# The first 384 tokens in tiles of 128 queries with all heads, up to product 1, and key zeros written by the evacuations

## The chip, the cores and the metric

One core of a Trainium2 chip. The metric is the device time of one execution in microseconds (us). The fast executions of one kernel lie within about 1.3% of each other here; runs that came out over 1.5% above the fastest of the same kernel are called slow. No ratio below uses them.

Names in the views: PE is TensorE (the matmuls), PEld its weight loads, DVE VectorE, ACT ScalarE, POOL GpSimd. Matmuls and transposes write into PSUM; an evacuation is a copy out of it. A load lands when its last byte has arrived and whoever waits for it is released.

## The reference, cut to what matters

Eight heads of causal attention over 768 tokens, four batches, head size 64. Heads 0, 2 and 6 see every earlier token; the others see the first four tokens (the sinks) and a window of 64. The result, 3072 tokens of 512 values, goes through two products with a leaky ReLU between them.

```python
scores = q @ k.T / sqrt(64)             # per batch and head
keep   = causal, or causal & (sink | in_window) for heads 1, 3, 4, 5, 7
x      = (softmax(where(keep, scores, -1e9)) @ v).transpose(0, 2, 1, 3).reshape(3072, 512)
h      = x @ w_in                       # product 1: 512 -> 2048
out    = maximum(0.01 * h, h) @ w_out   # product 2: 2048 -> 512
```

## The kernel before

It works through eight chunks of 384 tokens. While TensorE does the products of one chunk, the attention of the next is threaded into them. Only the first chunk has no products to hide behind, and its front is what the change rewrites. Keys are kept as `kt[partition, pair, head in pair, token]`: two heads share the 128 partitions, and the half that belongs to the other head must be zero, so that one matmul can contract over 128 partitions.

```python
def turn_pair(n, p, tags, engs, nms="kq"):       # one pair of heads, 384 tokens
    ...                                          # three transposes into PSUM tile pt
    if nm == "k":
        for hh in range(2):
            r = slice(64 * hh, 64 * hh + 64)     # only the head's own half
            move(kt[i][r, p, hh, CH * c : CH * c + CH], pt[r, 0:3, :])
    else:
        move(qx[n][:, p, :], pt[:, 0:3, :])

def zero_keys(i, eng, lo, hi):                   # the other halves
    for hh in range(2):
        eng.memset(kt[i][64 - 64 * hh : 128 - 64 * hh, :, hh, lo:hi], 0.0)

for p in range(2):
    load_pair("k", nc.sync, p)                   # heads 0 to 3 as fp32 pairs
    load_pair("q", nc.scalar, p)
make_identity(nc, ident)
load_three("k", nc.gpsimd, 4, 8)                 # heads 4 to 7 as bf16
load_three("q", nc.gpsimd, 4, 8)
...
for i in range(2):
    nc.vector.memset(va[i][:, :, :, D], 1.0)     # the ones column of v: first on DVE
nc.vector.memset(shift[:], 0.0)
nc.vector.tensor_copy(ident_f[:], ident[:])
zero_keys(0, nc.vector, 0, CH)
... # masks on POOL
load_v(0, (0,))                                  # after the ones in program order
...
zero_keys(1, nc.gpsimd, 0, CH)
...
turn_pair(0, 0, ("py", "py"), "va")              # then scores, exp, mask, v by head
...
p0 = in_slots(0)                                 # product 1 of the first chunk:
run(p0[0:1])                                     # 16 blocks of 4 matmuls of 384 columns
```

`va` is the v tile: 65 columns for each head, 64 of v and one of ones, which gives the sum of the softmax with the same matmuls. A load of v and the memset of the ones write different bytes of the same tile. `move` copies from PSUM with DVE ("v") or ACT ("a").

The softmax here doesn't subtract the row's maximum and nothing guards it: scores larger than these inputs give would overflow.

Of the kernel before, what the change touches and what calls it, by code (L numbers as in the profile page):

```python
# [21 lines left out]
def kernel(  # L22
# [36 lines left out]
    def bank(tag, shape, dtype):  # L59
        return ps.tile(shape, dtype, name=tag, tag=tag, bufs=BANKS[tag])  # L60

    def bf(name, *shape):
        return one.tile([128, *shape], BF16, name=name)

    wide = {nm: ap.rearrange("b h (c p g) d -> b c p h (g d)", g=3, p=128) for nm, ap in (("q", q), ("k", k))}
    nat = {nm: ap.rearrange("b h (c g p) d -> b c p h g d", g=3, p=128) for nm, ap in (("q", q), ("k", k), ("v", v))}
    q_k = {nm: ap[0, :, 0:CH].rearrange("h (g p) d -> p h g d", p=128) for nm, ap in (("q", q), ("k", k))}
    w_in_r = moe_w_in.rearrange("(g p) n -> p g n", p=128)
    w_out_r = moe_w_out.rearrange("(g p) n -> p g n", p=128)

    ident = bf("ident", 128)
    ident_f = one.tile([128, 128], FP32, name="ident_f")
    m_caus = bf("m_caus", 128)
    m_one = bf("m_one", 64)
    m_win = bf("m_win", 6, 64)
# [6 lines left out]
    vs = [bf(f"vs{i}", H, D + 1) for i in range(2)]  # L82
    ksink = [bf(f"ksink{i}", 4 * SK) for i in range(2)]
    ats = [bf(f"ats{i}", 3, 4, 64) for i in range(5)]
    w_in_bf = bf("w_in_bf", KG, DF)
    w_out_bf = bf("w_out_bf", NG, DM)


    raw = {}

    three = {}

    def load_three(nm, eng, lo, hi):
        t = one.tile([128, hi - lo, 3 * D], BF16, name=f"{nm}w{lo}")
        for h in range(lo, hi):
            three[nm, h] = t[:, h - lo]
        eng.dma_start(out=t[:], in_=wide[nm][0, 0, :, lo:hi])

    def load_pair(nm, eng, p):
        t = one.tile([128, 3, 2, D], FP32, name=f"{nm}f{p}")  # L100
        three[nm, p, "f"] = t
        for hh in range(2):
            eng.dma_start(out=t[:, :, hh], in_=q_k[nm][:, 2 * p + hh])

    def load_qk(n, nms="kq"):
        b, c = ORDER[n]
# [6 lines left out]
    def load_v(n, gs=range(3)):  # L113
        b, c = ORDER[n]
        for g in gs:
            nc.gpsimd.dma_start(out=va[b][:, 3 * c + g, :, 0:D], in_=nat["v"][b, c, :, :, g])  # L116
# [3 lines left out]
    def load_sinks(b):  # L120
        vsf[b] = rot.tile([32, D], FP32, name="vsf", tag="vsf", bufs=2)
        nc.sync.dma_start(out=vsf[b][:], in_=v[b, :, 0:NS, :])
# [9 lines left out]
    def load_in(c0, c1):  # L132
        nc.gpsimd.dma_start(out=w_in_bf[:, :, c0:c1], in_=w_in_r[:, :, c0:c1])
# [9 lines left out]
        eng.dma_start(out=vb[i][0:64, lo:hi], in_=va[i][64:128, lo:hi])  # L143
        eng.dma_start(out=vb[i][64:128, lo:hi], in_=va[i][0:64, lo + 1 : hi + 1])

    def v_shift_pe(t, tag, eng, b=0):
        s = bank(tag, [128, 512], FP32)
        w = 7 * (D + 1)
        for e in range(2):
            nc.tensor.matmul(s[:, 0:w], lhsT=shift[:, e, :], rhs=va[b][:, t + e, 1:H, :],  # L150
                             start=(e == 0), stop=(e == 1))
        dst, src = vb[b][:, t, 1:H, :], s[:, 0:w].rearrange("p (h d) -> p h d", h=7)
        if eng == "v":
            nc.vector.tensor_copy(dst, src)  # L154
        else:
            nc.scalar.activation(out=dst, in_=src, func=ACTF.Copy)
# [6 lines left out]
    def zero_keys(i, eng, lo, hi):  # L163
        for hh in range(2):
            eng.memset(kt[i][64 - 64 * hh : 128 - 64 * hh, :, hh, lo:hi], 0.0)  # L165

    def zero_small(i, eng):
        eng.memset(ksink[i][:], 0.0)
        eng.memset(vs[i][:], 0.0)
# [9 lines left out]
            return qx[n][:, g, p, lo - 128 * g : hi - 128 * g]  # L179
        return qx[n][:, g : hi // 128, p, :]  # L180

    def turn_pair(n, p, tags, engs, nms="kq"):
        b, c = ORDER[n]
        i = b % 2
        if n not in qx:
            qx[n] = rot.tile([128, 4, CH], BF16, name="qt", tag="qt", bufs=2)
        for nm, tag, eng in zip(nms, tags, engs):
            f = n == 0 and p < 2
            pt = bank(tag, [128, 4, 128], FP32 if f else BF16)
            for g in range(3):  # L190
                if f:
                    nc.tensor.transpose(pt[:, g, :], three[nm, p, "f"][:, g], ident_f[:])
                elif n == 0:
                    for hh in range(2):
                        nc.tensor.transpose(pt[64 * hh : 64 * hh + 64, g, :],
                                            three[nm, 2 * p + hh][:, D * g : D * g + D], ident[:])
                else:
                    nc.tensor.transpose(pt[:, g, :], raw[nm, n][:, g, 2 * p : 2 * p + 2, :], ident[:])

            def move(dst, src):  # L200
                if n == 0 and not f:
                    src = src.rearrange("p g t -> p t g")
                    dst = dst.rearrange("p (t g) -> p t g", g=3)
                else:
                    dst = dst.rearrange("p (g t) -> p g t", g=3)
                if eng == "v":
                    nc.vector.tensor_copy(dst, src)
                else:
                    nc.scalar.activation(out=dst, in_=src, func=ACTF.Copy)

            if nm == "k":
                for hh in range(2):
                    r = slice(64 * hh, 64 * hh + 64)
                    move(kt[i][r, p, hh, CH * c : CH * c + CH], pt[r, 0:3, :])
            else:
                move(qx[n][:, p, :], pt[:, 0:3, :])

    def turn_dma(n):
        qx[n] = rot.tile([128, 3, 4, 128], BF16, name="qd", tag="qd", bufs=3)
# [44 lines left out]
    def sink_keys(b):  # L264
        for f in sink_keys_by(b):
            f()
# [168 lines left out]
            return r  # L435


    gs = {}
    py = {}

    def in_slots(n, tags=("ph",)):
        def tick(t):
            if t == 0:
                gs[n] = rot.tile([128, NG, CH], BF16, name="g", tag="g", bufs=2)
            ph = bank(tags[t % len(tags)], [128, 512], FP32)
            for g in range(KG):
                nc.tensor.matmul(ph[:, 0:CH], lhsT=w_in_bf[:, g, 128 * t : 128 * t + 128],  # L447
                                 rhs=xts[n][:, g, :], start=(g == 0), stop=(g == KG - 1))
            nc.scalar.activation(out=gs[n][:, t, :], in_=ph[:, 0:CH], func=ACTF.Prelu, alpha=0.01)  # L449

        return [lambda t=t: tick(t) for t in range(NG)]

    def out_slots(n, tags=("py", "py", "py"), halves=False):
        slots = []
# [25 lines left out]
    def run(*lists):  # L480
        for l in lists:
            for f in l:
                f()

    def merge(ms, as_):

        r, done = [], 0
        for j, m in enumerate(ms):
            want = (j + 1) * len(as_) // len(ms)
            r += as_[done:want] + [m]  # L490
            done = want
        return r + as_[done:]


    for p in range(2):
        load_pair("k", nc.sync, p)
        load_pair("q", nc.scalar, p)
    make_identity(nc, ident)
    load_three("k", nc.gpsimd, 4, 8)
    load_three("q", nc.gpsimd, 4, 8)  # L500
    load_sinks(0)
    load_sinks(1)
    for i in range(2):
        nc.vector.memset(va[i][:, :, :, D], 1.0)
    nc.vector.memset(shift[:], 0.0)
    nc.vector.tensor_copy(ident_f[:], ident[:])
    zero_keys(0, nc.vector, 0, CH)
    for a in ats:
        nc.vector.memset(a[:, :, 1:3, :], 0.0)
    nc.scalar.activation(out=shift[:, 0, 0:64], in_=ident[:, 64:128], func=ACTF.Copy)  # L510
    nc.scalar.activation(out=shift[:, 1, 64:128], in_=ident[:, 0:64], func=ACTF.Copy)
    nc.gpsimd.memset(m_caus[:], 1.0)
    keep(m_caus[:], [[1, 128]], ALU.is_ge, 0, -1)
    load_v(0, (0,))
    nc.gpsimd.memset(m_one[:], 1.0)
    keep(m_one[:], [[-1, 64]], ALU.is_gt, 0, 1)
    keep(m_one[:], [[1, 64]], ALU.is_ge, 64, -1)
    load_v(0, (1, 2))
    load_in(0, 512)
    nc.gpsimd.memset(m_sink[:], 1.0)  # L520
    keep(m_sink[:], [[-NS, H]], ALU.is_ge, 0, 1)
    keep(m_sink[:], [[NS, H]], ALU.is_ge, NS - 1, -1)
    zero_small(0, nc.gpsimd)
    load_qk(1)
    zero_keys(1, nc.gpsimd, 0, CH)
    zero_small(1, nc.gpsimd)
    load_in(512, 1024)
    load_v(1)
    load_in(1024, 1536)
    load_in(1536, 2048)  # L530
    for i in range(3):
# [2 lines left out]
    load_out(3)  # L534
    load_v(2)

    a0 = Attention(0, ("psS", "ph"), ("po", "po", "py", "py"))
    R0, S1, R2, S3, S4, S5, R6, S7 = (a0.units[h] for h in range(H))

    def qk(*us):  # L540
        run([x[0] for x in us])

    def av(*us):
        run([x[1] for x in us])

    turn_pair(0, 0, ("py", "py"), "va")
    nc.vector.tensor_copy(m_win[:], m_one.rearrange("p (o t) -> p o t", o=1).to_broadcast([128, 6, 64]))
    nc.vector.tensor_copy(m_win0[:, 1:], m_win[:, 1:])
    nc.vector.tensor_copy(m_win0[:, 0, :], m_caus[:, 0:64])
    nc.vector.memset(m_win0[0:NS, 1, :], 1.0)  # L550
    qk(*R0)
    qk(*S1)
    turn_pair(0, 1, ("po", "po"), "av")
    turn_pair(0, 2, ("py", "py"), "va")
    qk(*R2)
    qk(*S3)
    turn_pair(0, 3, ("po", "po"), "av")
    sink_keys(0)
    qk(*R6)
    qk(*S4)  # L560
    v_shift_pe(0, "ph", "a")
    v_shift_pe(1, "psS", "v")
    av(*R0)
    qk(*S5)
    a0.sink()
    sink_values(0, nc.vector)
    nc.vector.tensor_copy(vs[0][0:32, :, D], m_sink[0:32, :])
    av(*R2)
    qk(*S7)
    av(*S1)  # L570
    xs0 = a0.finish(0)
    av(*S3)
    xs1 = a0.finish(1)
    av(*R6)
    av(*S4)
    av(*S5)
    xs2 = a0.finish(2)
    av(*S7)
    xs3 = a0.finish(3)
    a0.x_t(0, xs0, "ph")  # L580
    turn_pair(1, 0, ("psS",), "a", "k")
    a0.x_t(1, xs1, "ph")
    turn_pair(1, 1, ("psS",), "v", "k")
    a0.x_t(2, xs2, "ph")
    a0.x_t(3, xs3, "ph", "v")
    p0 = in_slots(0)
    run(p0[0:1])
    turn_pair(1, 0, ("psS",), "v", "q")
    turn_pair(1, 1, ("psS",), "a", "q")
    run(p0[1:2])  # L590
    turn_pair(1, 3, ("psS", "psS"), "va")
    run(p0[2:3])
    a1 = Attention(1, po_tags=("po", "po", "po", "py"), xt_eng="v").slots([0, 2, 6, 1, 3, 4, 5, 7])
    run(a1[0:2])
    turn_pair(1, 2, ("py", "py"), "va")
    sink_keys(1)
    sink_values(1, nc.vector)
    nc.vector.tensor_copy(vs[1][0:32, :, D], m_sink[0:32, :])


    shifts = [lambda: v_shift_pe(0, "ph", "v", 1), lambda: v_shift_pe(1, "ph", "v", 1)]
    run(p0[3:4], merge(p0[4:8], a1[2:7] + shifts[0:1] + a1[7:8] + shifts[1:]), merge(p0[8:12], a1[8:-3]), merge(p0[12:], a1[-3:]))
    zero_keys(0, nc.vector, CH, S)
    zero_keys(1, nc.vector, CH, S)
    for i in range(2, B):
# [72 lines left out]
```

## Time and profile before

| | before |
|---|---|
| time, median of 3 runs (range) | 242.64 us (242.45 to 243.33) |
| span of the profiled run | 241.4 us |
| first transpose | 4.33 us |
| first matmul of product 1 | 22.68 us |
| product 1 of the second 384 tokens begins ("the join") | 42.4 us |

In the slices of the span (40 of 6.0 us; a digit is the busy share in tenths), TensorE is less than 90% busy only in the first five, in one near the middle and in the last:

```profile
PE   2787899999999999899999999999999999999994
```

In the timeline, each line is: start in us, duration of one or of the whole group in us, engine, line and operation, what it writes and reads, how many; in brackets how long the engine stood before it and for what. Two lines of the kernel before: the ones of the v tile are the first thing on DVE, and the first load of v comes behind them:

```profile
1.05 0.31 DVE L504 MEMSET va<- 128x48 bf16 x2 [1.05 <-PEq L659]
...
3.67 0.90 POOL L116 DMA_DIRECT2D va<-in_v_dram  x1
```

The other views of the kernel before stand in the prediction.

### The profile page before, as it was taken

To read this page: it belongs to the slowest core of one execution; us is meant where nothing else is said; L and a number is where in the kernel's file an instruction comes from. 1 tells how busy PE (TensorE), PEld (TensorE's weight loads), DVE (VectorE), ACT (ScalarE), POOL (GpSimd) and SP (SyncE) were. 2 spreads that over 40 slices of the span, in tenths; PEclk is the share of its full clock that TensorE was granted. 3 is DMA by queue.
4 is the path that set the end of the run, shared out by engine and by line. 5 is a ranking of instruction groups with operands and counts; after the bars stand their busy time and mean duration, and the time that the engine had idled before them with its cause. 6 is when DMAs were issued, how large, how long until landed. Compare 5 with 4: busy or idle time off the path is not lost.

```text
span 241.4 us, 4947 instructions
## 1 busy us (share of the span) xinstructions
PE 226.1 (94%) x1980; PEld 137.0 (57%) x1980; DVE 97.6 (40%) x267; ACT 130.2 (54%) x286; POOL 74.6 (31%) x98
## 2 busy tenths in 40 slices
PE   2787899999999999899999999999999999999994
PEld 2555566554556567565656655666556665555553
DVE  6667547405254537327712671234511441111121
ACT  3664865660665687665436553766556764433300
POOL 8999734119239007705900840000000000000000
PEclk9999999999999999999999999999999999999999
DMA  7999999999999995996998999751210111111112
GB/s 127 184 162 114 190 207 176 178 151 151 138 187 206 191 182 35 141 177 140 133 148 129 188 172 105 159 124 30 69 55 7 61 35 60 43 43 46 42 45 87
DMA packets 107334, 29.08 MB, mean 120 GB/s; under 512 B 99248, under 2 KB 103600, under 8 KB 107312
## 3 DMA queue, kind: packets, MB, share of 16 engines
q0 software_dynamic: 73920, 13.24, 69.9%
q1 hardware_dynamic: 31792, 15.15, 31.0%
q10 hardware_dynamic: 1600, 0.39, 0.8%
q8 instruction: 15, 0.25, 0.4%
q14 instruction: 7, 0.06, 0.1%
HBM read 27.30 MB, written 6.29 MB: 139 GB/s over the span
## 4 chain that ended last, share of the span: by engine, by line
PE 83%; POOL 7%; DVE 4%; ACT 3%; DMA 1%; issue 1%; DVEq 0%; POOLq 0%
PE ph L447 34%; PE py L460 29%; PE po L292 6%; PE psS L323 5%; PE psS L460 4%; PE psS L358 2%; PE psS L303 2%; DMA out_dram<-o 1%; POOL kt L165 1%; POOL qb L111 1%; POOL kb L111 1%; POOL va L116 1%; ACT ats L363 1%; ACT xt L403 1%; PE psS L401 1%
## 5 line engine op out<-in xcount | busy, mean ns | idle before, releaser
L447 PE MATMUL ph<-xt,w_in_bf 128*128 128x384 bf16 x512 | 101.9, 325 | 0.4 <-DVE vb L154 0.3
L449 ACT ACTIVATE g<-ph 128x384 bf16<-128x384 f32 x128 | 63.0, 492 | 60.4 <-PE ph L447 59.5
L460 PE MATMUL py<-w_out_bf,g 128*128 128x512 bf16 (+1 forms) x352 | 91.0, 374 | 0.0
L447 PEld LDWEIGHTS <-w_in_bf 128*128 128x128 bf16 x512 | 46.6, 97 | 33.6 <-issue 2.2
L460 PEld LDWEIGHTS <-g 128*128 128x128 bf16 x400 | 35.4, 97 | 25.9
L328 ACT ACTIVATE at<-psS 128x384 bf16<-128x384 f32 x81 | 38.5, 491 | 16.2 <-PE psS L323 16.1
L466 DVE COPY o<-py 128x512 f32<-128x512 f32 (+1 forms) x22 | 14.9, 678 | 52.1 <-PE py L460 50.7
L111 POOL DMA_DIRECT2D kb<-in_k_dram x21 | 18.6, 895 | 32.8 <-DMA kd<-kb 32.1
L323 PE MATMUL psS<-qd,kt 128*128 128x384 bf16 (+2 forms) x90 | 22.9, 293 | 0.0
L367 DVE TENSOR_TENSOR ats<-ats,m_win 128x384 bf16<-128x384 bf16 x40 | 15.1, 377 | 17.7 <-ACT ats L363 17.3
L116 POOL DMA_DIRECT2D va<-in_v_dram x24 | 21.3, 910 | 2.4 <-DMA w_out_bf<-in_moe_w_out_dram 1.8
L292 PE MATMUL po<-va,at 128*128 128x65 bf16 x240 | 20.3, 195 | 1.4 <-DVE at L333 1.1
L363 ACT ACTIVATE ats<-psS 128x384 bf16<-128x384 f32 x38 | 18.5, 490 | 5.2 <-PE psS L358 4.9
L292 PEld LDWEIGHTS <-at 128*128 128x128 bf16 x252 | 16.2, 99 | 7.4 <-DVE at L333 1.5
L111 POOL DMA_DIRECT2D qb<-in_q_dram x21 | 18.6, 908 | 5.3 <-DMA w_out_bf<-in_moe_w_out_dram 2.4
L391 DVE TENSOR_TENSOR xs<-po,linv 128x384 bf16<-128x384 f32 x29 | 16.2, 557 | 1.0
L358 PEld LDWEIGHTS <-kt 128*128 128x128 bf16 x240 | 12.9, 102 | 6.5 <-issue 0.4
L333 DVE TENSOR_TENSOR at<-at,m_caus 128x128 bf16<-128x128 bf16 x24 | 5.6, 231 | 25.6 <-ACT at L328 25.5
L323 PEld LDWEIGHTS <-kt 128*128 128x128 bf16 x108 | 10.4, 99 | 9.4 <-issue 1.9
L231 DVE COPY kt<-kd 64x512 bf16<-64x512 bf16 x36 | 13.5, 374 | 0.6
L292 PEld LDWEIGHTS <-ats 128*128 128x128 bf16 x240 | 11.2, 97 | 4.0 <-DVE ats L367 0.8
L331 DVE TENSOR_TENSOR at<-at,m_caus 128x256 bf16<-128x256 bf16 x24 | 7.0, 291 | 14.2 <-ACT at L328 14.2
(107 smaller groups left out, 168.1 us busy)
## 6 DMA issues: line engine op xcount, KB each, us to landing
out_dram<-o SPq DMA_DIRECT2D x23, 256.0 KB, 3.6
va<-in_v_dram POOLq DMA_DIRECT2D x24, 128.0 KB, 6.9
kb<-in_k_dram POOLq DMA_DIRECT2D x21, 128.0 KB, 5.6
qb<-in_q_dram POOLq DMA_DIRECT2D x21, 128.0 KB, 5.8
w_in_bf<-in_moe_w_in_dram POOLq DMA_DIRECT2D x4, 512.0 KB, 7.4
w_out_bf<-in_moe_w_out_dram POOLq DMA_DIRECT2D x4, 512.0 KB, 12.7
vb<-va SPq DMA_DIRECT2D x8, 195.0 KB, 3.7
vb<-va SPq DMA_DIRECT2D x4, 130.0 KB, 3.1
```

Of the source, the lines that this page charges most:

```text
L111: nc.gpsimd.dma_start(out=t[:, g], in_=nat[nm][b, c, :, :, g])
L116: nc.gpsimd.dma_start(out=va[b][:, 3 * c + g, :, 0:D], in_=nat["v"][b, c, :, :, g])
L292: nc.tensor.matmul(o, lhsT=lhsT, rhs=rhs, start=first, stop=False, skip_group_check=True)
L323: nc.tensor.matmul(s[:, off : off + w], lhsT=kt[i][:, p, hh, 128 * kj : 128 * kj + 128], rhs=q_of(n, p, lo, CH), start=(j == 0), stop=(j = ...
L328: nc.scalar.activation(out=a[:, 0:off], in_=s[:, 0:off], func=ACTF.Exp, scale=SM)
L358: nc.tensor.matmul(s[:, 64 * m : 64 * m + 64], lhsT=kt[i][:, p, hh, k0 : k0 + 128], rhs=q_of(n, p, 64 * m, 64 * m + 64), start=(m == 0), s ...
L363: nc.scalar.activation(out=av_, in_=s[:, 0:CH].rearrange("p (j e f) -> p j e f", j=3, e=2), func=ACTF.Exp, scale=SM)
L367: nc.vector.tensor_mul(av_, av_, m_)
L391: nc.vector.tensor_tensor(xs[:], po[:, :, :, 0:D], linv.to_broadcast([128, 3, 2, D]), op=ALU.mult)
L447: nc.tensor.matmul(ph[:, 0:CH], lhsT=w_in_bf[:, g, 128 * t : 128 * t + 128], rhs=xts[n][:, g, :], start=(g == 0), stop=(g == KG - 1))
L449: nc.scalar.activation(out=gs[n][:, t, :], in_=ph[:, 0:CH], func=ACTF.Prelu, alpha=0.01)
L460: nc.tensor.matmul(py[n][:, 0 : c1 - c0], lhsT=gs[n][:, ng, 128 * tt : 128 * tt + 128], rhs=w_out_bf[:, ng, c0:c1], start=(ng == 0), stop= ...
```

## The change

The intent is a shorter front. The first 384 tokens are taken in three tiles of 128 queries, each with all eight heads, so that product 1 of tile 0 can begin before tiles 1 and 2 are through. Tile 0 of k and q comes as fp32 for all heads and is cast; the other tiles come as bf16. Thirteen matmuls on zeros (`idle`) are to warm TensorE. The zeros of the keys are no longer written by memsets: an evacuation of k copies the full 128 partitions, once for each head of the pair, multiplied by a per-partition scalar that is 1 on the head's own half and 0 on the other. The core of the diff:

```diff
-    for p in range(2):
-        load_pair("k", nc.sync, p)
-        load_pair("q", nc.scalar, p)
+    load_first("k")
+    load_first("q")
+    load_v(0, (0,))
     make_identity(nc, ident)
-    load_three("k", nc.gpsimd, 4, 8)
-    load_three("q", nc.gpsimd, 4, 8)
+    load_tile(1)
+    load_v(0, (1,))
     load_sinks(0)
     load_sinks(1)
+    nc.vector.memset(blank[:], 0.0)
+    ... # half: ones on a head's own partitions, zeros on the other
     for i in range(2):
         nc.vector.memset(va[i][:, :, :, D], 1.0)
     nc.vector.memset(shift[:], 0.0)
-    nc.vector.tensor_copy(ident_f[:], ident[:])
-    zero_keys(0, nc.vector, 0, CH)
+    ... # zeros of the sink keys, sink values and two mask tiles
+    nc.vector.tensor_copy(k0[:, 0], f0["k"])
+    nc.scalar.activation(out=q0[:, 0], in_=f0["q"], func=ACTF.Copy)
...
-    zero_keys(1, nc.gpsimd, 0, CH)
...
+def move(eng, dst, src, hh=None):
+    if eng == "v" and hh is None:  nc.vector.tensor_copy(dst, src)
+    elif eng == "v":               nc.vector.tensor_scalar_mul(dst, src, half[:, hh : hh + 1])
+    ... # the same two on ACT, with scale=
...
-    turn_pair(0, 0, ("py", "py"), "va")
-    ... # four pairs, scores by head, v, transposes of x
+    idle("psS", 13)
+    turn_tile("k", 0, "va"); turn_tile("q", 0, "v"); turn_tile("k", 1, "va")
+    F0.all_heads(0, "psS"); F0.all_heads(1, "ph")
+    ... # F0, F1, F2: scores, exp, masks, v of tiles 0, 1, 2
+    F0.x_t("py", "a")
+    in_tile(0, 0)                  # product 1 of tile 0: 16 matmuls of 128 columns
+    ... # F1.x_t, in_tile(0, 1), F2.x_t, in_tile(0, 2), in_tile(1, 0) to (1, 2),
+    ... # the second 384 tokens' transposes among them; blocks 8 to 15 full width as before
```

## The prediction

> **What bounds the kernel now.** I read the page's busy shares first, then the chain of waits, then a table of four stretches, then the timeline of the first 45 us, because the diff ends where the product of the second 384 tokens begins.
>
> ```profile
> PE 226.1 (94%) x1980; PEld 137.0 (57%) x1980; DVE 97.6 (40%) x267; ACT 130.2 (54%) x286; POOL 74.6 (31%) x98
> ...
> PE 83%; POOL 7%; DVE 4%; ACT 3%; DMA 1%; issue 1%; DVEq 0%; POOLq 0%
> ```
>
> TensorE sets the end; 83% of the chain that ended last is matmul. The rest of the chain (POOL, DVE, ACT) lies at the front:
>
> ```profile
> 38.75 2.04 PE ph L447 x12
> 40.79 0.17 PE psS L401 x3
> 40.95 0.65 PE ph L447 x4
> 41.60 0.17 PE psS L401 x3
> 41.77 11.76 PE ph L447 x68
> 53.53 6.91 PE py L460 x32
> ```
>
> Of the 68 matmuls at 41.77 the first four (0.65 us) still belong to the first 384 tokens. The 64 behind them begin at 42.4: product 1 of the second 384 tokens. I call this point the join. From it on the two kernels have the same TensorE program.
>
> ```profile
> core 0: us, PE busy (x) PEld busy (x) DVE busy (x) ACT busy (x) POOL busy (x), PEclk, DMA share, GB/s
> 0.00:4.30 4.30, 0.00 (x0) 0.00 (x1) 2.72 (x11) 1.24 (x1) 3.44 (x11) 1.00 0.55 116
> 4.30:22.68 18.38, 14.02 (x158) 10.54 (x158) 13.16 (x38) 10.99 (x27) 18.00 (x28) 1.00 1.60 152
> 22.68:42.40 19.72, 17.89 (x198) 12.19 (x198) 11.28 (x36) 12.94 (x30) 10.81 (x14) 1.00 1.60 190
> 42.40:241.40 199.00, 194.20 (x1627) 114.23 (x1624) 70.43 (x185) 105.00 (x229) 42.32 (x48) 1.00 0.92 111
> ```
>
> After the join TensorE is busy 194.2 of 199.0 us. So the time is the join plus about 199 us, and only the moment of the join can change. The table splits the front in three: until the first transpose (4.3), until the first matmul of product 1 (22.68, 18.4 us later), and until the join (19.7 us later). The middle stretch is a relay between TensorE, DVE and ACT: in it DVE is busy 13.2 us.
>
> **What the Trainium skill says.** "TensorE: Matmul & The Clock Gate", part 1, says that the array starts at half clock, opens after about 3.4 us of sustained work and closes again after an idle window of about 3.4 us. The trace agrees with the first half:
>
> ```profile
> 15.99 0.54 PE L292 MATMUL po<-va,at 128*128 128x65 bf16 x6
> ...
> 17.12 0.34 PE L292 MATMUL po<-va,at 128*128 128x65 bf16 x6
> ```
>
> The same six matmuls cost 0.54 us and a moment later 0.34: the clock opened near 16.6 us, so the old front runs cold until then. The granted-clock column stays at 1.00 throughout and does not show it. The same page ("Architectural detail") says that ScalarE and VectorE queues are strict first-in first-out; the trace agrees in that DVE and ACT never start an instruction ahead of an earlier one. "DMA: Bandwidth & Descriptors" ("Anatomy of one DMA") says that a transfer's semaphore fires only when its last byte is confirmed. For the loads of v, which matter below, the tile view of the trace gives, from issue to landing:
>
> ```profile
> L116 POOL DMA_DIRECT2D va<-in_v_dram x6: 881/904/911, 3.7 to 21.1; - x6
> ...
> DMA to landing us min/median/max: 5.8/6.0/6.6
> ```
>
> **The change part by part.** Everything is ahead of the join.
>
> (a) The start. Heads 0 to 3 came as fp32 pairs and were transposed as fp32 from 4.33 us. Now tile 0 of k and q comes as fp32 for all heads, DVE casts k and ACT casts q, then come bf16 transposes. The load of v tile 0 is moved to the head of the POOL queue, v tile 1 stands fourth, and both are now ahead of the DVE memset that writes the ones column of the v tile. I looked at the semaphores in the built program: that memset, sixth on DVE, waits for the v tile 0 and the v tile 1 load (the bytes do not overlap, but the order is kept for the tile). In the old kernel it was reversed: the load waited for the memset, which ran at 1.05 us. DVE is in order, so the cast of k, seven places down, waits too. My estimate of when: POOL begins at about 0.75; 0.9 for v tile 0, 0.5 for the identity and its gaps, 2 x 0.9 for k and q tile 1, so v tile 1 is issued at about 4.0 and lands 6.0 later, at 10.0. Then DVE has the ones (0.31 for both tiles), shift (0.17), sink keys and values (0.3 + 0.5, by 0.9 ns an element as in the 128x768 memset of 0.70), two 128x256 memsets (0.54), and the cast of 128x512 (0.6): the cast ends at about 12.4. First transpose 12.4 against 4.33: **+8.1 us**. The 13 warm-up matmuls (256 columns, 0.21 us each cold = 2.8 us) run from about 1.3 to 4.1, then TensorE has nothing for 8 us; by the skill's rule it is cold again.
>
> (b) From the first transpose to the first matmul of product 1 (old: 18.4). Evacuations: ACT's 128x384 is 0.49 and 128x256 0.38, so 128x512 is 0.60; DVE's bf16 copy of 384 from PSUM is 0.36, so 512 is 0.45 (0.5 with the scalar); its multiply of 256 fp32 from PSUM 0.43, by 0.56 for 384. In DVE's order from the cast on: five memsets 1.05; k0 0.5, q0 0.45; k1 stands until its PSUM buffer is free, which needs ACT's half of k0, and this waits for DVE's half (both write one tile): 0.95, then 0.5; sink keys and window masks 1.25; mask, q1, mask 0.36 + 0.45 + 0.49 with 0.5 of waits for exp; two masks 0.36 + 0.42 and 1.1 waiting for scores and exp; two reciprocals and multiplies 1.2; mask 0.2; k2 0.5; sink values 0.9; q2 0.45: 11.8 us. Behind it on TensorE and ACT, cold: av of tile 1 (10 matmuls, 0.9), scores of tile 2 (0.6 + 0.45), av (0.95), scores (1.2), transposes (0.4), ACT's copy (0.6) and hops (0.3): 5.4. Sum 17.2. Against 18.4: **-1.2 us**. What it removes is real but small here: DVE's two zeroings of keys (2 x 0.70), POOL's 2.8 us, and the sink values' wait for POOL.
>
> (c) From there to the join (old: 19.7). Old, the whole of 384 queries stood ready at 22.68; new, only tile 0. Six blocks of 16 matmuls of 128 columns at about 0.06 us are 6.0 us, with their copies of xt (0.6 each, ACT, between exp and Prelu) between the first three. Tile 2's av (23 matmuls, 1.0), and 24 transposes of the second 384 tokens (1.5 to 2 with their PSUM waits), whose evacuations (DVE 3 x 0.75 + 2 x 0.37, ACT 2 x 0.98) are the relay before the first scores. Sum about 11.9 to the first full-width block. Then 8 blocks of 0.65 = 5.2 and the rest of that attention, about 4.9 of matmul by its columns, plus 1.2 of tail waits: 11.3. Sum 23.2: **+3.5 us**.
>
> Sum 8.1 - 1.2 + 3.5 = 10.4, join at about 52.8. A relay worked out link by link overlaps less than the machine does, so I take off 2: join at 50.8, time 242.6 + 8.4 = **251 us**.
>
> **The rivals.** First, that the wait in (a) is short or hidden: v tile 1 lands at 8 rather than 10. For it: the DMA engines carry fewer bytes ahead of it than before. Against: the six v loads took 5.8 to 6.6. It gives 249. If DVE did not stand at all, the cast would end near 5.3 (the first fp32 pair landed at 4.3), k and q tile 1 land at about 8.5 to 9, just when needed, and the time would be 244, or 242 with the array kept warm. Second, that finer tiles overlap so well that the middle shortens by 5 us or more, which the author must have meant: then the stall is all but paid for, 245. Against: DVE's own work in (b) is 11 us and the chain goes through it. Third, that the transfers become the bound after the join: the k and q of the third chunk reuse buffers that are now free some 8 us later. In the old kernel POOL's wait for the transposed keys ended at 53.4 and DVE first used them at 57.6, 4.2 us of slack, and join and loads move together, so I expect nothing; if not, 254. Fourth, that POOL, whose third v load waits for the same memset, holds back the first weights: issued at about 11.2 they land near 18.6 (7.4 as in the old kernel), long before 29. Nothing.
>
> **Range and chances.** 246.5 to 255.5: low for rival two in part, high for no overlap at all and rival three. Faster by over 2% (under 237.8) needs the join at 37.6; from a start of 12.4 with some 20 us of DVE and TensorE relay and 10 us of matmul behind it, I give it 0.04. Within 2% (up to 247.5): 0.15. Slower: 0.81.
>
> **What would show it.** The DVE memset of the ones column at about 10 us with a wait of some 8 us on a v load; the first k transpose at 12 to 13; TensorE idle from 4 to 12; the first 128-wide product 1 block near 29; the 64-matmul run of the second 384 tokens beginning at 49 to 54; after it the same 199 us. It is wrong if the ones are written before 5 us, or if the join lies under 46.

## The result, and the profile after

| | before | after |
|---|---|---|
| time, median of 4 runs each on one chip (range) | 242.99 us (242.45 to 244.78) | 249.87 us (248.88 to 250.44) |
| ratio of fast runs | 1 | 1.0266 (95%: 1.0201 to 1.033) |
| span of the profiled run | 241.4 us | 248.4 us |
| first transpose | 4.33 us | 11.85 us |
| first matmul of product 1 | 22.68 us | 25.76 us |
| the join | 42.4 us | 48.99 us |
| join to end | 199.0 us | 199.4 us |

The changed kernel is slower by 2.7%. A ratio, here and below, is the mean time of one kernel's fast runs over the mean of the other's fast runs of the same rounds, so it is not quite the ratio of the medians beside it.

The page of the changed kernel: the busy shares of the engines, then the slices of TensorE and of its granted clock, then the shares of the chain that ended last.

```profile
PE 227.4 (92%) x2048; PEld 141.1 (57%) x2048; DVE 96.9 (39%) x274; ACT 129.6 (52%) x280; POOL 73.7 (30%) x98
...
PE   4067789899999999999999999999999999999993
...
PEclk9998899999999999999999999999999999999999
...
PE 86%; DVE 5%; ACT 4%; DMA 2%; POOL 1%; issue 1%; POOLq 0%; DVEq 0%
```

TensorE is busy 1.3 us longer than before but the span is 7.0 us longer, so nearly all of the loss is TensorE standing. The slices show where: 4, then 0, where the kernel before had 2, 7. The first slice is higher only because the matmuls on zeros count as busy. Total busy shares of DVE and ACT are no guide: they hardly moved.

The stretches of the prediction, at the new borders (core line as in the prediction: from and to, length, then busy us of each engine with its instructions, granted clock, DMA share and GB/s):

```profile
core 0: us, PE busy (x) PEld busy (x) DVE busy (x) ACT busy (x) POOL busy (x), PEclk, DMA share, GB/s
0.00:11.85 11.85, 2.96 (x14) 1.81 (x14) 2.44 (x14) 1.91 (x2) 9.06 (x20) 1.00 1.27 114
11.85:25.76 13.91, 10.04 (x112) 8.55 (x113) 10.29 (x34) 8.23 (x18) 13.37 (x20) 0.91 1.80 158
25.76:48.99 23.23, 20.42 (x300) 16.59 (x299) 14.17 (x42) 14.56 (x31) 9.87 (x12) 0.98 1.61 189
48.99:248.40 199.41, 194.03 (x1627) 114.17 (x1624) 70.00 (x185) 104.90 (x229) 41.36 (x47) 1.00 0.84 106
```

Against the kernel before (4.33, 18.35, 19.72 and 199.00 us, with the start counted to the first transpose): the start is 7.5 us longer, the middle 4.4 us shorter, the stretch to the join 3.5 us longer, and the rest the same to 0.4 us. In the first stretch DVE is busy only 2.44 us of 11.85. The timeline of the start says why:

```profile
1.13 2.96 PE L146 MATMUL psS<-blank 128*128 128x256 bf16 x13 [1.13 <-DVE blank L615]
...
4.65 0.89 POOL L113 DMA_DIRECT2D va<-in_v_dram  x1
...
9.52 0.31 DVE L620 MEMSET va<- 128x48 bf16 x2 [8.20 <-DMA va<-in_v_dram]
...
9.91 0.88 POOL L113 DMA_DIRECT2D va<-in_v_dram  x1 [1.36 <-DVE va L620]
...
11.25 0.54 DVE L625 CAST k<-o 128x512 bf16<-128x512 f32 x1
...
11.85 0.61 PE L212 MATMUL py<-ident,k 128*128 128x128 bf16 x4 [7.76 <-POOL m_sink L637]
```

The memset of the ones, 0.31 us of work, stands 8.20 us for a load of v. DVE takes its instructions in order, so the cast of k waits too, and TensorE stands 7.76 us after its matmuls on zeros. The bracket of the last line names POOL as the releaser of TensorE. That is an inference that misleads: POOL's instruction does nothing for a transpose of k; what TensorE needed was the cast at 11.25. The weight loader's own wait (8.2 us, for the cast of k) names the right one. The chain of waits of the changed kernel now runs through that load, and later reaches the run of 68 matmuls, whose last 64 begin the second chunk:

```profile
4.65 4.56 DMA va<-in_v_dram
...
48.34 11.76 PE ph L546 x68
```

### The profile page after: what moved, and what is told of

It is laid out like the page before. It is cut to its first block, busy times and chain, and to the rows that moved or that the text cites. A ratio compares the mean times of both kernels' runs of the same rounds, so it can differ in the third digit from the quotient of the medians.

```text
span 248.4 us, 5068 instructions
## 1 busy us (share of the span) xinstructions
PE 227.4 (92%) x2048; PEld 141.1 (57%) x2048; DVE 96.9 (39%) x274; ACT 129.6 (52%) x280; POOL 73.7 (30%) x98
## 4 chain that ended last, share of the span: by engine, by line
PE 86%; DVE 5%; ACT 4%; DMA 2%; POOL 1%; issue 1%; POOLq 0%; DVEq 0%
PE ph L546 31%; PE py L572 29%; PE po L294 6%; PE psS L325 5%; PE psS L572 3%; PE ph L559 3%; PE psS L360 2%; DMA va<-in_v_dram 2%; PE psS L305 2%; PE psS L403 1%; ACT kt L193 1%; ACT ats L365 1%; PE po L505 1%; DVE vs L681 1%; ACT g L562 0%
## 5 line engine op out<-in xcount | busy, mean ns | idle before, releaser
L546 PE MATMUL ph<-xt,w_in_bf 128*128 128x384 bf16 x480 | 95.5, 326 | 0.0
L548 ACT ACTIVATE g<-ph 128x384 bf16<-128x384 f32 x120 | 58.9, 491 | 58.3 <-PE ph L546 57.6
L546 PEld LDWEIGHTS <-w_in_bf 128*128 128x128 bf16 x480 | 43.7, 97 | 31.5 <-issue 1.3
L330 ACT ACTIVATE at<-psS 128x384 bf16<-128x384 f32 x78 | 37.0, 490 | 15.5 <-PE psS L325 15.3
L365 ACT ACTIVATE ats<-psS 128x384 bf16<-128x384 f32 x35 | 17.0, 489 | 4.5 <-PE psS L360 4.1
L294 PEld LDWEIGHTS <-at 128*128 128x128 bf16 x234 | 15.1, 98 | 5.6 <-DVE at L333 0.6
L369 DVE TENSOR_TENSOR ats<-ats,m_win 128x384 bf16<-128x384 bf16 x35 | 12.5, 357 | 14.7 <-ACT ats L365 14.5
L393 DVE TENSOR_TENSOR xs<-po,linv 128x384 bf16<-128x384 f32 x27 | 15.0, 557 | 0.9
L360 PEld LDWEIGHTS <-kt 128*128 128x128 bf16 x210 | 10.8, 98 | 6.2 <-issue 0.4
L325 PEld LDWEIGHTS <-kt 128*128 128x128 bf16 x99 | 9.5, 97 | 7.0 <-issue 0.4
L294 PE MATMUL po<-va,ats 128*128 128x65 bf16 x116 | 11.3, 194 | 0.7 <-DVE xs L393 0.7
## 6 DMA issues: line engine op xcount, KB each, us to landing
w_out_bf<-in_moe_w_out_dram POOLq DMA_DIRECT2D x4, 512.0 KB, 12.2
```

Of the source, the lines that this page charges most:

```text
L294: nc.tensor.matmul(o, lhsT=lhsT, rhs=rhs, start=first, stop=False, skip_group_check=True)
L325: nc.tensor.matmul(s[:, off : off + w], lhsT=kt[i][:, p, hh, 128 * kj : 128 * kj + 128], rhs=q_of(n, p, lo, CH), start=(j == 0), stop=(j = ...
L330: nc.scalar.activation(out=a[:, 0:off], in_=s[:, 0:off], func=ACTF.Exp, scale=SM)
L360: nc.tensor.matmul(s[:, 64 * m : 64 * m + 64], lhsT=kt[i][:, p, hh, k0 : k0 + 128], rhs=q_of(n, p, 64 * m, 64 * m + 64), start=(m == 0), s ...
L365: nc.scalar.activation(out=av_, in_=s[:, 0:CH].rearrange("p (j e f) -> p j e f", j=3, e=2), func=ACTF.Exp, scale=SM)
L393: nc.vector.tensor_tensor(xs[:], po[:, :, :, 0:D], linv.to_broadcast([128, 3, 2, D]), op=ALU.mult)
```

## The experiments

All twelve kernels gave a correct result, and all were timed in five rounds against the kernel before on the same chip. "The front" below is the three marks: first transpose, first matmul of product 1, join. They come from the one profiled run of each kernel.

### Taking the wait away, and putting it into the other kernel

**1. The ones first.** One move: the memset ahead of every load of v, as in the kernel before. Only the order changes; the memset itself stays.

```diff
+    for i in range(2):
+        nc.vector.memset(va[i][:, :, :, D], 1.0)
     load_first("k")
     load_first("q")
     load_v(0, (0,))
 ...
-    for i in range(2):
-        nc.vector.memset(va[i][:, :, :, D], 1.0)
     nc.vector.memset(shift[:], 0.0)
```

> The changed kernel with one thing undone: the two DVE memsets of the ones columns stand ahead of the loads of v again, so that no memset waits for a load. Theory A (the DVE queue standing 8.2 us behind the v loads is the whole loss): the first k transpose moves from 11.85 us to about 5, the first product 1 block from 25.8 to about 19, the join from 49.0 to about 42, time 242 to 243.5, ratio to the kernel before 0.995 to 1.005. Rival B (finer tiles themselves cost, and the stall only hid the wait for the k and q tiles 1 and 2): the middle stretch grows because those tiles land at 9 to 11 us, join at 45 or later, time 245 to 247.

Measured: the front is 4.30, 19.96, 42.8. The timeline of DVE in this kernel:

```profile
1.05 0.31 DVE L608 MEMSET va<- 128x48 bf16 x2 [1.05 <-PEq L777]
...
3.81 0.43 DVE L625 CAST k<-o 128x512 bf16<-128x512 f32 x1 [0.56 <-DMA o<-in_k_dram]
```

The join is 6.2 us earlier than in the changed kernel. The times fell into two groups: three fast runs (243.4 to 244.3) with the ratio 0.9985 (0.992 to 1.0049), and four slow ones near 247.7. (The kernel before had one slow run, 248.94, among its eleven of these rounds.) The profiled run is one of the slow group, so it says nothing of the fast runs after the join; what it shows is a new wait of its own there, for the store of an output tile and for what DVE delivers behind it:

```profile
DVE o L578 <- DMA out_dram<-o: 3.8, 1, 3.8
PE psS L403 <- DVE xs L393: 3.3, 2, 2.9
```

(The columns are: total us waited, times, longest.) What follows, from the fast runs: the wait explains the loss, and the finer tiles without it give parity, not a gain.

**2. The same without the matmuls on zeros.**

```diff
-    idle("psS", 13)
```

> As the run with the ones first, and the 13 warm-up matmuls taken out. If they buy an open array clock for the first tiles, the matmuls of the first scores take 0.63 us for four instead of about 0.39 and the time is 0.5 to 2 us longer than with them; if the first scores are at half clock in both, no difference (within 0.3%).

Measured: 244.53 us (243.45 to 244.86), six fast runs, ratio 1.0016 (0.9977 to 1.0055); front 4.39, 19.15, 42.1. There was no slow group. The first four scores of 128 columns took 0.63 us here and in experiment 1 alike. So in the profiled run of experiment 1 the fill had not sped up the array by the time real work came. That differs from run to run: the same fill stands in experiments 5 and 10 below, and in their profiles these scores took 0.39 us. The lines of experiment 1 and of experiment 5:

```profile
7.84 0.63 PE L462 MATMUL psS<-qt,kt 128*128 128x128 bf16 x4
```

```profile
7.83 0.39 PE L463 MATMUL psS<-qt,kt 128*128 128x128 bf16 x4
```

It did not last (the next such group, near 10.7 us, took 0.58 and 0.59), and neither kernel is faster for it. With and without it the fill gained nothing.

**3. The changed kernel without the matmuls on zeros**, the wait left in.

```diff
-    idle("psS", 13)
```

> The changed kernel with the 13 warm-up matmuls alone taken out. By the prediction they are wasted behind the stall (TensorE has nothing from 4.1 to 11.85 us): 249.5 to 250.5, the same as the changed kernel. Rival: they still shorten the time to the opening of the clock, 251 or more.

Measured: 249.34 us (249.04 to 250.02), ratio 1.0225 (1.0188 to 1.0263); front 11.66, 25.38, 48.2. The intervals of the ratio overlap with that of the changed kernel. The fill is neither the loss nor a gain.

**4. The wait put into the kernel before.** In the kernel before, the same memset is moved behind its first load of v, and nothing else changes.

```diff
-    for i in range(2):
-        nc.vector.memset(va[i][:, :, :, D], 1.0)
 ...
     load_v(0, (0,))
+    for i in range(2):
+        nc.vector.memset(va[i][:, :, :, D], 1.0)
```

> The kernel before with the stall alone put in: its two memsets of the ones columns are written after the load of v tile 0, so DVE waits for that load (landing near 10.3 us) before its first evacuation of k at 5.24, and POOL's next v loads wait for DVE. Theory A: the old front is a chain from that evacuation on, so most of 5 us shows, join 46 to 47.5, time 246.5 to 248. Rival (the old front has slack, because its sink values waited for POOL until 17.7 us): under 2 us, 243 to 245.

Measured: 249.59 us (248.77 to 251.43; five fast runs, and one slow one of 252.91), ratio 1.0248 (1.0197 to 1.03). The timeline of DVE, where the first evacuation of k stood at 5.24 us in the kernel before:

```profile
10.52 0.75 DVE L207 CAST kt<-py 64x384 bf16<-64x384 f32 x1 [6.04 <-issue]
10.58 0.31 DVE L514 MEMSET va<- 128x48 bf16 x2
```

(Here the profile has the wait as "issue" and puts it down to the instruction that stands a moment ahead; the memset is ahead in program order.) The front is 4.39, 27.22, 47.2: the join is 4.8 us later. That is what was expected, but the time is 1.6 to 3.1 us above what was expected. The rest came after the join, 202.2 us against 199.0, with the wait for the store of an output tile at 3.2 us where the kernel before has 1.1. So one misplaced memset costs the old kernel as much as the whole change cost, though a part of it through a collision later.

**9. Waiting for tile 0 of v alone.** In the changed kernel, v tile 1 is loaded later, behind the memset; the memset now waits for the first load of the queue only.

```diff
     load_tile(1)
-    load_v(0, (1,))
 ...
     load_tile(2)
+    load_v(0, (1,))
     load_v(0, (2,))
```

> The changed kernel with the load of v tile 1 moved behind the second k and q tiles, so that the ones memset waits for v tile 0 alone (issued first, at 1.32 us). It tells which of the two loads sets the 8.2 us. If tile 1, issued at 4.65 and landing near 9.2, sets it and tile 0 lands at about 5, the first k transpose comes at about 7.5 and the time is 245 to 246.5. If tile 0 itself lands only at 8 to 9 because all early loads share the DMA engines, 248.5 to 250, the changed kernel's time.

Measured: 245.35 us (245.24 to 245.46), ratio 1.0074 (1.0047 to 1.0101). The timeline of DVE:

```profile
6.07 0.31 DVE L619 MEMSET va<- 128x48 bf16 x2 [4.76 <-DMA va<-in_v_dram]
```

The wait is 4.76 us instead of 8.20, the front is 8.23, 21.41, 44.2, and from the join to the end it takes 199.6 us. Of the two loads it was the later, v tile 1, that set the 8.20 us, and a dose of 3.4 us less wait takes 4.8 us off the join. (The 1.4 us beyond the dose are not explained by a run of their own; a small copy on DVE that takes 1.35 us in the changed kernel took 0.17 here, see the last section.)

### What is left once the wait is gone

Without the wait the join lies where it lay before, at 42 to 43 us. The four kernels here ask why not earlier, and why the time is not even a little better.

**5. Four output tiles instead of three**, on top of experiment 1, against the wait for the store (two tiles of scores share a buffer to make room).

```diff
-    ... name="o", tag="o", bufs=3)
+    ... name="o", tag="o", bufs=4)
+    share = bf("share", 10, 128)          # at8 of tile 0 and at_first of tile 2
```

> The ones first, and four output tiles of 128x512 in place of three (room for it by letting two score tiles of the first 384 tokens share one buffer). In the run with the ones first DVE waited 3.8 us near 73 to 77 us for a store of an output tile, TensorE stood 2.9 us behind it, its clock fell to 0.53 for some 3 us, and 4 of 7 executions took 247.6 us instead of 243.4 to 244.3. Theory: this one wait makes both the slow executions and 1 to 2 us of the fast ones. Then no execution is over 244, the wait for the store is gone, and the ratio to the kernel before is 0.985 to 0.995. Rival: the clock falls for another reason, and a second group of executions 3 to 4 us longer stays.

Measured: 243.63 us (242.94 to 244.36), ratio 1.0017 (0.999 to 1.0044), front 4.29, 19.02, 42.0. No slow run in six. But experiments 2 and 8, with three output tiles, had none either, though the same wait stands in their profiles (2.8 and 2.0 us against 3.8), so that the wait made the slow group of experiment 1 is not shown. The fast runs gained nothing: that half of the expectation failed. The wait for the store is no longer in the list of waits, and another stands there that the kernel before does not have among its longer ones, for the transposed keys:

```profile
DVE kt L233 <- DMA kd<-kb: 4.0, 2, 3.6
```

From the join to the end it takes 200.7 us, 1.7 more than before.

**6. The activation table early**, on top of experiment 5: ACT's first instruction is moved to the start by a copy of one column, so that the load of its table (1.28 us at 4.35 in experiment 1) is over before the cast of q.

```diff
+    early = bf("early", 2)
+    nc.vector.memset(early[:], 1.0)
 ...
+    nc.scalar.activation(out=early[:, 0:1], in_=early[:, 1:2], func=ACTF.Copy)
```

> As the run with four output tiles, and a one-column activation on ScalarE before it waits for q, so that the 1.28 us table load (which stood between the landing of q at 4.35 and the cast of q at 5.65) is done early. If that load is on the path, the first scores start about 1.2 us earlier and the join and the time are 0.8 to 1.3 us less than in the run without it. Rival: k and q tile 1 land at 7.2 to 9, and the gain is lost in that wait: under 0.3 us.

Measured: 244.34 us (243.23 to 244.76), ratio 1.004 (1.0009 to 1.007), front 4.64, 18.81, 42.0. The rival was right: it gains nothing. The list of waits has 0.5 us of TensorE's for the second part of the first weights.

**8. Product 1 of the first chunk at full width**, on top of experiment 1: the three tiles of attention stay, but product 1 waits for all three and runs in blocks of 384 columns, as before.

```diff
-    in_tile(0, 0)          # and (0, 1), (0, 2), (1, 0), (1, 1), (1, 2)
+    p0 = in_slots(0)
+    run(p0[0:4])           # after the third tile; then p0[4:7] and p0[7:8]
```

> The ones first, and product 1 of the first 384 tokens at full width (128x384 blocks, as in the kernel before) behind the last of the three tiles, instead of tile by tile: the first part of the change without the last. The matmul columns are the same. If the tile-wise product fills waits of the relay, taking it away costs 1 to 2.5 us: 244.5 to 246. If it is what stretches the way from its first block to the join (22.8 us against 19.7 in the kernel before), taking it away gains about 1 us: 242 to 243.

Measured: 243.65 us (243.26 to 245.43), ratio 1.0032 (0.9999 to 1.0064), front 4.38, 22.14, 41.8. Product 1 begins 2.2 us later than in experiment 1, yet the join is not later. Starting product 1 on tile 0 early does not bring the join forward.

**10. The weights earlier**, on top of experiment 6: the third quarter of w_in is loaded ahead of the second half of the first batch's v.

```diff
     load_in(512, 1024)
+    load_in(1024, 1536)
     load_v(1)
 ...
-    load_in(1024, 1536)
```

> The run with four output tiles and the early table, with the third quarter of the first weights loaded ahead of the second chunk's v instead of behind it. In that run the first full-width block of product 1 began at 31.0 us and the chain of waits gave 12.9% of its first 60 us to the load of these weights, so that starting earlier gained nothing. If the weights are the bound there, the join comes 0.5 to 1.2 us earlier and the time is 242.3 to 243.3, ratio 0.997 to 1.001. Rival: v, now later, or the transposed keys after the join take its place: no difference.

Measured: 243.78 us (243.21 to 245.65), ratio 1.0028 (0.9992 to 1.0064), front 4.54, 19.80, 42.6. No difference, as the rival said.

### The other half of the change by itself

**7. The kernel before with zeros written by the evacuations.** Nothing of the tiles: only the multiplication by the half mask, and the memsets of key zeros for the first chunks of batches 0 and 1 taken out.

```diff
     if nm == "k":
         for hh in range(2):
-            r = slice(64 * hh, 64 * hh + 64)
-            move(kt[i][r, p, hh, CH * c : CH * c + CH], pt[r, 0:3, :])
+            move(kt[i][:, p, hh, CH * c : CH * c + CH], pt[:, 0:3, :], hh)
 ...
-    zero_keys(0, nc.vector, 0, CH)
 ...
-    zero_keys(1, nc.gpsimd, 0, CH)
```

> The kernel before with the second half of the change alone: the evacuations of transposed k write the zero halves of the keys (a per-partition scale of 1 or 0), the four zeroing memsets of keys on DVE and POOL are gone. In the kernel before the sink values waited for POOL's two memsets of keys (1.4 us each) until 17.67 us, and TensorE stood 1.0 us before 18.8. Theory: without them product 1 begins 0.8 to 1.3 us earlier, time 241.5 to 242.3, ratio 0.994 to 0.998. Rival: the next wait (exp, masks) takes its place, no difference.

Measured: 241.62 us (240.95 to 242.64), ratio 0.9942 (0.9913 to 0.9972), front 4.06, 22.32, 41.8, from the join to the end 199.0 us as before. This beats both kernels. The timeline of POOL in the kernel before:

```profile
12.17 2.65 POOL L111 DMA_DIRECT2D qb<-in_q_dram  x3
14.86 2.80 POOL L165 MEMSET kt<- 64x1536 bf16 x2
17.61 0.54 POOL L168 MEMSET ksink<- 128x544 bf16 x1
```

and with the zeros written by the evacuations:

```profile
12.15 2.65 POOL L112 DMA_DIRECT2D qb<-in_q_dram  x3
14.75 0.62 POOL L169 MEMSET ksink<- 128x544 bf16 x1
```

POOL's 2.80 us are gone, and the loads of weights and of v that it issues behind them come 2.9 us earlier (15.71 for 18.58, 16.46 for 19.33). The join of the profiled run comes 0.6 us earlier (0.27 us of it at the first transpose already), and from there to the end nothing changes. The ratio amounts to 1.4 us; no trace shows where the rest is, and which of the removed memsets brings the gain was not separated. DVE's sink values, which the prediction held to wait for POOL's memsets, did not: they ran at 17.68 us before and at 17.65 here.

**11. The same with four output tiles.**

```diff
-                o = rot.tile([128, DM], FP32, name="o", tag="o", bufs=3)
+                o = rot.tile([128, DM], FP32, name="o", tag="o", bufs=4)
```

> The kernel before with the zeros written by the evacuations, and four output tiles of 128x512 in place of three. The kernel before has 1.1 us of DVE wait for the store of an output tile and little of it reaches TensorE (its waits after the join sum to 1.2 us). Expected the same as with the zeros alone within 0.3%: 241.2 to 241.8, perhaps with fewer executions over 242.5. Faster than both kernels in any case.

Measured: 242.58 us (241.62 to 243.54), ratio 0.9961 (0.9928 to 0.9995). Not told apart from experiment 7.

**12. The same with a filled start.** Thirteen matmuls on zeros ahead of the first transposes and two behind them, so that TensorE has no gap from 1.1 to 6 us.

```diff
+    idle(13)
     turn_pair(0, 0, ("py", "py"), "va")
+    idle(2)
```

> As the run before it, with 13 matmuls of zeros (256 columns) ahead of the first transposes and 2 more in TensorE's wait behind them. In the kernel before the array runs at half clock until about 16.6 us. If sustained work in the first 6 us opens it, the scores of the first heads (0.48 to 0.53 us each) fall to about 0.33 and product 1 begins 0.5 to 1.5 us earlier: 240 to 241. If it stays at half clock, as in the run of the new kernel with and without its 13 matmuls, nothing, or 0.2 us longer.

Measured: 242.10 us (240.75 to 242.48), ratio 0.9933 (0.9902 to 0.9963). The intervals of experiments 7, 11 and 12 overlap, so the fill is not shown to gain. Its profile is of use all the same. It opened the clock, for a moment: the score of 384 columns at 6.18 us took 0.32 us, and the next of that shape 0.50, as much as both took in the kernel before (0.48 and 0.50).

```profile
6.18 0.32 PE L336 MATMUL ph<-qt,kt 128*128 128x384 bf16 x1 [0.15 <-DVE kt L219]
...
10.20 0.50 PE L336 MATMUL psS<-qt,kt 128*128 128x384 bf16 x1
```

The table of stretches of this kernel has the granted clock in the column after POOL:

```profile
4.00:6.00 2.00, 1.99 (x9) 1.53 (x9) 1.00 (x2) 1.10 (x4) 1.86 (x5) 1.00 1.20 156
6.00:8.00 2.00, 0.82 (x11) 0.62 (x10) 1.72 (x8) 1.39 (x4) 1.95 (x4) 1.00 1.53 200
8.00:10.00 2.00, 1.42 (x18) 1.04 (x17) 0.66 (x2) 1.05 (x2) 1.91 (x5) 0.86 2.35 159
10.00:12.00 2.00, 2.00 (x27) 1.39 (x23) 1.65 (x5) 1.69 (x5) 2.00 (x3) 0.50 1.57 195
```

From 6 to 8 us TensorE was busy for 0.82 us of 2, and a little later the clock stood at half. A filled start does not last through the relay behind it.

## Why the prediction was right or wrong

The time, 251.0 us, was 1.1 us above the median of 249.87, inside the range, and "slower" held. The reason for it, the memset behind the loads of v, is what the runs show. Point by point:

- **(a) The start, +8.1 us predicted, +7.5 measured.** The wait of "some 8 us" was 8.20, and it was on v tile 1: experiment 9 takes that load out of the wait and 3.4 us of it go. Two errors offset each other in part: the load was issued at 4.65 rather than 4.0, and landed 4.56 us later rather than the 6.0 of the six v loads in the old profile; why it was faster no run shows. From the memset to the first transpose it took 2.33 us, with 2.4 predicted. Experiments 1 and 2 (the wait taken out: parity) and 4 (the wait put into the old kernel: +2.5%) show that the order of one memset carries the sign of the result.
- **(b) The middle, −1.2 us predicted, −4.4 measured. This is the step that was mis-sized.** Its sum was 17.2 us and the stretch took 13.9. The evacuation of q of tile 2, the end of the part summed on DVE, ended 10.6 us after the first transpose (11.8 predicted), and from there to product 1 it took 3.3 us (5.4 predicted). The second term was priced as if TensorE were cold throughout and as if the first half of tile 1's v had still to be done. In the profile, eight of the ten matmuls of that half had run between 20.2 and 22.1 us, before that evacuation ended, and the clock was open from some point between 19.3 and 20.0 until about 23.3 us: eight scores took 0.39 us for four, against 0.63 before and after. The stall itself helped the middle: in experiment 1, without it, TensorE waits 1.41 us for ACT's cast of q between its first two groups of transposes, and the middle is only 2.7 us shorter than in the kernel before; in the changed kernel that cast was long done. (The prediction's terms on DVE also add up to 11.6, not 11.8.)
- **(c) To the join, +3.5 us predicted, +3.5 measured.** 23.2 us predicted, 23.23 measured; also by its parts: 11.9 to the first full-width block and 11.3 behind it were predicted, 12.2 and 11.1 measured.
- **The 2 us taken off for overlap.** They were not placed in any step. They belonged in (b), which was 3.3 us too long; with the 0.6 us of (a) the sum of the steps was 10.4 against 6.6 measured, and the deduction made up for half of the error. That the total came within 1.1 us is partly luck.
- **After the join**, 199 us predicted, 199.4 measured: what the old and the new kernel share is the same.
- **The signs.** The memset came at 9.52 us with its wait, TensorE stood from 4.1 to 11.85, both as said. The first block of product 1 was to come near 29 and came at 25.76 (step b). The join was to lie at 49 to 54 and lay at 48.99, a hair below. The first k transpose was to come at 12 to 13, and came at 11.85.
- **Two readings.** The prediction says that the trace never shows an instruction of DVE starting ahead of an earlier one. By the recorded starts it does, by a little: in the kernel before a mask product (7.54 us) stands ahead of a memset (7.72) that comes first in the program. For waits of microseconds, as here, the order held. The memset that gave 0.9 ns an element is 64x768, not 128x768.

Of the rivals: the first said that without the wait the time would be 244, or 242 "with the array kept warm". Experiments 1, 2 and 5 gave 243.6 to 244.5, so the first figure held; the second did not, since no fill tried here kept the array warm. The second, a middle shorter by 5 us or more, came near (4.4), but the stall and step (c) together were 11 us, so it was far from paying. The third, transfers that bind after the join, did not occur in the changed kernel, but longer waits stand in experiments 1, 4 and 5, where the join to end took 203.2 (a slow run), 202.2 and 200.7 us with waits for the store or for transposed keys (in 1 and 4 the granted clock also fell behind the wait, to 0.53 from 78 to 80 us and 0.76 from 80 to 84; in 5 it stayed at 1.00 there). The fourth was right: POOL's third v load stood 1.36 us for the memset, and no wait for weights of any size appears.

Why the finer tiles gain nothing even without the wait: in experiment 1 (its profile is of a slow run, but what is slow there begins at 74 us) the start is that of the kernel before, the middle is 2.7 us shorter (15.66 against 18.35) and the stretch to the join 3.1 us longer (22.86 against 19.72). Product 1 of tile 0 begins while tiles 1 and 2 still need the same DVE and ACT (in that profile TensorE waits 0.69 and 0.61 us for ACT's copies of xt ahead of the second and third tile), and experiment 8 shows that the early beginning can be given up at no cost. What is shorter comes back before the join; which engine brings it back was not tested by itself.

What stays open: why the kernels with the wait removed take 0.4 to 2 us longer after the join than the kernel before, though their TensorE program is the same there. The new wait differs from kernel to kernel, and the effect does not follow the time of the join: 199.6 us in experiment 9, with the join at 44.2, 201.1 in experiment 2 with 42.1. Each of these is one profiled run, and the six fast runs of experiment 2 alone lie 1.4 us apart, so part of it may be spread. One waiting transfer was removed (experiment 5), and another took its place. The loss of about 1 us within (b) that the last section tells was not tested by itself either.

## What to carry to other kernels

In an in-order queue the place of a tiny initialisation counts more than its length: a memset ordered behind a load into the same tile, even of other bytes, hands what is left of that load's latency to everything behind it. So write constants into a tile before the first load into it, and when a change moves loads to the front, look at what now stands behind them. A finer split of a pipeline's first stage is worth only what moves the point where the steady part begins; measure that point, and test each half of a change alone, for here the small half gained 0.6% and the large half hid it.

## What the Trainium skill lacked or had wrong

- "TensorE: Matmul & The Clock Gate", part 1 and its summary: it says that about 3.4 us of sustained work opens the clock, and in its advice that gaps over about 3 us close it; a second failure mode, by many small idles, it names without numbers of how many. The first agrees here: behind 13 matmuls (2.96 us) and the first transposes, together 3.4 to 3.7 us of work, the clock was open in the profiles of experiments 5 and 10 (four scores in 0.39 us) and still at half in those of 1, 6 and 8 (0.63); with two matmuls more (1.1 to 6 us, experiment 12) it was open. The second is too mild: in experiment 12 no gap from 6 to 10 us was over 1.03 us, TensorE was busy 0.82 of 2 us in the first half, and the clock was at 0.50 by 10 us. In the changed kernel gaps of 1.39 and 0.36 us stood before the fall; the table of stretches and two groups of the same shape show it:

```profile
20.00:22.00 2.00, 0.61 (x13) 0.51 (x12) 2.00 (x6) 1.13 (x2) 2.00 (x4) 1.00 1.90 156
22.00:24.00 2.00, 1.64 (x34) 1.54 (x32) 1.45 (x6) 1.02 (x2) 1.94 (x4) 0.82 1.39 192
24.00:26.00 2.00, 2.00 (x17) 1.41 (x15) 1.27 (x5) 1.71 (x5) 2.00 (x4) 0.50 2.27 162
```

```profile
22.78 0.39 PE L479 MATMUL ph<-qt,kt 128*128 128x128 bf16 x4
...
23.90 0.63 PE L475 MATMUL ph<-qt,ksink 128*128 128x128 bf16 x4
```

- The same page ("Seeing it yourself") warns that clock events in a trace can be unreliable; it does not say that the granted-clock column can read 1.00 from the start while the array is still at half clock. In the kernel before it reads 1.00 while six matmuls take 0.54 us that take 0.34 a moment later; go by durations of one shape.
- "SBUF — State Buffer", "Who interferes with whom": it says that VectorE copies in a two-port mode and GpSimd share a port pair, and that the second to issue blocks until the first is done. Here the length of the block fits, the order does not, and the price can be two GpSimd instructions long. In the changed kernel a copy of 32x8 took 1.35 us, and ended at 22.45, with the second of two POOL memsets (22.42); in experiment 3 it took 1.37, and ended 22.28 against 22.25. In the kernel before it took 0.45, and ended 18.66 against 18.62; in experiment 7, where POOL was past these memsets by then, 0.17. With only DMA issues beside it, it took 0.17 us (experiment 9) to 0.53 (experiment 1). By the recorded starts the copy of the changed kernel (21.10) stands ahead of both memsets (21.37 and 21.86), while POOL was still issuing a load, so that it lost the port pair to them is inferred from where it ends. No experiment was made for it. DVE, in the changed kernel:

```profile
21.10 1.35 DVE L681 COPY vs<-m_sink 32x8 bf16<-32x8 bf16 x1
21.17 1.28 DVE L187 COPY qt<-py 128x512 bf16<-128x512 bf16 x1
```

  and POOL:

```profile
21.37 0.58 POOL L170 MEMSET ksink<- 128x544 bf16 x1
21.86 0.56 POOL L171 MEMSET vs<- 128x520 bf16 x1
```

- No page says that a memset and a load of other bytes of one tile are kept in program order; here that order alone cost 8.20 us of DVE's time.
